# Second layers of eight chunks as seven block products, in a phase of their own

## The chip, the cores and the metric

The kernel runs on one core of a Trainium2 chip. TensorE multiplies matrices into PSUM, VectorE and ScalarE move and combine data, GpSimd does small element-wise work, and SyncE (SP) issues nearly all transfers between HBM and SBUF. The metric is the time of one execution in device microseconds (us), as a median of several runs, lower is better.

## What is computed

A linear attention with positive random features, followed by a gated two-layer network:

```python
def phi(x):
    proj = np.einsum('bhsd,df->bhsf', x, w_phi)
    proj = proj - np.max(np.abs(proj), axis=-1, keepdims=True)
    return np.concatenate([np.exp(proj), np.exp(-proj)], axis=-1)
q_p, k_p = (phi(q), phi(k))
kv = np.einsum('bhsf,bhsd->bhfd', k_p, v)
z = np.sum(k_p, axis=2)
num = np.einsum('bhsf,bhfd->bhsd', q_p, kv)
den = np.einsum('bhsf,bhf->bhs', q_p, z)[..., None] + 1e-06
x = (num / den).transpose(0, 2, 1, 3).reshape(4608, 512)
...
g = x @ w_gate
silu = g * (1.0 / (1.0 + np.exp(-g)))
val = x @ w_val
return (silu * val @ w_out).astype(np.float32)
```

Sizes: 8 batches, 8 heads, 576 tokens, head size 64, 128 features; then 4608 tokens, 512 inputs, 1536 hidden columns, 512 outputs. The three weight matrices arrive as 64-bit floats.

## The kernel before

**Numbers.** TensorE gets float32 operands in a form that is fast but keeps fewer bits (F32R). Each operand is split into a high part and a low remainder: ScalarE casts the high part (`copy` into `hh`, `xh`), VectorE subtracts (`hl`, `xl`). A product is then three matmuls: high by high, high by low, low by high.

**Tiling.** The 4608 tokens are 12 chunks of 384 (`CH`, `NCH`). The hidden columns are 12 groups of 128 (`NFT`, index `f`). For a chunk and an `f`, the first layer makes a gate and a value tile of 128 hidden columns by 384 tokens; tanh (ScalarE) and two VectorE operations make the hidden tile. The second layer (`second`, L864) takes 128 tokens of a hidden tile as the stationary operand and the 512 columns of `w2` for that `f` as the moving one, for three row tiles, and sums over `f` in three PSUM banks; behind `f` = 11 ScalarE copies a bank out (L905) and SP stores it.

**Stages.** Attention runs pair of heads by pair of heads (32 of them); its TensorE work goes ahead, and the network's matmuls fill the rest. Chunks 0 to 3 do their first layers directly (`first`, 24 matmuls of 384 columns for each `f`). Their sums for the block form below are made by `sums_of_weights` (L944).

Chunks 4 to 11 are taken in pairs by `pair` (L1054). Its first layer treats the two chunks, the two halves of the 512 inputs, and gate and value as a 2 x 2 block product, and makes it with seven block products instead of eight (products 0 to 6, line L1075, six matmuls of 384 columns each). `operands` (L1015) makes the seven left operands from four loads of `x_dram`, and `load_unit` (L999) fetches the weight blocks, in high and low, from `w1_dram` into six half buffers of `w1`, four loads for each `f`. The partial results live in two banks, `ps_gv`, with copies in `snap` (ScalarE L1083, VectorE L1086).

Pairs 4-5 and 6-7 are "narrow": between the products of the first layer stand the second layers of the first chunk only; the hidden tiles of the other chunk are stored in `h_dram` (`keep`, L843) and its second layers come behind the pair, from reloaded tiles. Pairs 8-9 and 10-11 are "wide": six banks hold the outputs of both chunks, whose second layers follow at once. `second` needs `w2_lo` for each `f`, reloaded by `parts_of_weights` (L788) into five buffers.

**Order.** All instructions are first collected as steps with costs and dependencies, and `Plan.run` (L101) lays them out ahead of time: on each engine the ready step of lowest rank goes first. Steps of the network on ScalarE, VectorE and SP mostly have the rank `FIRST`, preparations `NEXT`; TensorE's network products (`product`, L773) form one chain. `ahead(us)` holds a load back until that much planned TensorE work is left before its user. On the chip each queue is in order: a transfer that waits on SP holds back all transfers behind it.

**The early weights.** `weight_piece` (L350) turns the 64-bit weights into float32, splits them, and stores them: for the first layer the whole value (`w1_whole`) and both parts, for the second layer the low part (`w2_dram`); the high part of `w2` stays in SBUF (`w2_hi`).

Of the kernel before, what the change touches and what calls it, by code (L numbers as in the profile page):

```python
# [2 lines left out]

# [14 lines left out]
P = 128  # L18
# [31 lines left out]
NARROW = 2  # L50
AHEAD = (10, 8, 8, 20)
# [139 lines left out]
AT_ONCE = 2  # L191
# [28 lines left out]
def favor_attention_moe(ctx: ExitStack, tc: tile.TileContext, qT, kT, v, w_phi, wg, wv, wo, out):  # L220
# [8 lines left out]
    w2_dram = tc.dram_tile([NFT, P, DM], F32, name="w2_dram")  # L229
    h_dram = tc.dram_tile([NCH, NFT, P, CH], F32, name="h_dram")  # L230
# [10 lines left out]
    w2_hi = sb("w2_hi", [P, DM], F32R, NFT)  # L241
    w2_lo = sb("w2_lo", [P, DM], F32R, W2_SETS)
# [47 lines left out]
    hh, hl = sb("hh", [P, CH], F32R, 2), sb("hl", [P, CH], F32R, 2)  # L290
# [21 lines left out]
    ps_all = ps_o + work  # L312
# [37 lines left out]
    def weight_piece(f, layer, rank, over):  # L350
# [513 lines left out]
    def second(c, f, hidden, low, parts_of=range(NT), base=0, tail=None):  # L864
        b, ready = hidden
        readers, lo, lo_ready = low
        for t in parts_of:
            sl = slice(t * P, (t + 1) * P)
            o = ps_all[base + t]

            def go(t=t, sl=sl, o=o):
                if t == 0:
                    open_sum.append(f)
                    if f == NFT - 1:
# [5 lines left out]
                                            *(stored.get(base + t, ()) if f == 0 else ())])  # L880
# [8 lines left out]
            if n == NCH * NT - 1:  # L889
                for k, eng in enumerate(("ACT", "DVE")):  # L890
                    cols = slice(k * DM // 2, (k + 1) * DM // 2)

                    def copy(k=k, cols=cols, o=o):
                        if k:
                            nc.vector.tensor_scalar(out=tail[1][k](), in0=o[:, cols], scalar1=0.5, scalar2=None, op0=ALU.mult)
                        else:
                            nc.scalar.activation(tail[1][k](), o[:, cols], AF.Copy, scale=0.5)

                    cp = add(eng, act(DM // 2), copy, [done], FIRST)
                    q = nc.sync if k else nc.scalar  # L900
                    add("SP" if k else "ACT", P * DM * 2 if k else 60,
                        lambda q=q, k=k, cols=cols, rows=rows: q.dma_start(rows(cols), tail[1][k]()), [cp], FIRST)
                continue
            u = osb[n % len(osb)] if tail is None else tail[0][base + t]
            cp = add("ACT", act(DM), lambda o=o, u=u: nc.scalar.activation(get(u), o, AF.Copy, scale=0.5),  # L905
                     [done, out_done.get(n - len(osb)) if tail is None else None], FIRST)
            stored[base + t] = [cp]
# [12 lines left out]
    def tiles(c, f, hidden, low, base=0, tail=None):  # L920
        return [(c, f, hidden, low, range(t, t + 1), base, tail) for t in range(NT)]
# [50 lines left out]
    for c in range(EARLY, PAIRS):  # L972
        for f in range(NFT):
# [5 lines left out]
    ended = last["end"]  # L979
    x_half = lambda t, n: t[:, 2 * n:2 * n + 2]  # L980
    set2 = (PAIRS - 1) % X_SETS
    s0, s1_ = ((set2 + n) % X_SETS for n in (1, 2))
    op_hi = [x_half(xh[s0], 0), x_half(xh[s0], 1), x_half(xh[s1_], 0), x_half(xh[s1_], 1), view("m5", [2, CH], F32R, 1),
             x_half(xh[set2], 0), x_half(xh[set2], 1)]
    op_lo = [x_half(xl[s0], 0), x_half(xl[s0], 1), x_half(xl[s1_], 0), x_half(xl[s1_], 1), spare_lo,
             x_half(xl[set2], 0), x_half(xl[set2], 1)]
    snap = sb("snap", [P, CH], F32, 3)
    outs = [view("m2", [DM], F32, 2, DM * n) for n in range(2 * NT)]
    last_half = [view("m2", [DM // 2], F32, 2, 2 * NT * DM + n * DM // 2) for n in range(2)]

    op_free = [list(x_free[PAIRS - 3 + n]) for n in (0, 0, 1, 1)] + [list(early_done)] + [list(x_free[PAIRS - 1]) for _ in range(2)]
# [5 lines left out]
    held, loaded = {}, [0]  # L997

    def load_unit(f, j):  # L999
        u = UNITS[j]  # L1000
        g = u // 2
        if (f, g) not in held:
            first_ = 3 if g == 1 else 2 * g
            n = 2 * g + 2 - first_
            k = loaded[0] % len(slots)
            loaded[0] += 1
            after, slot_free[k] = slot_free[k], []
            stored_ = w_stored[f, 0 if g < 2 else g]
            held[f, g] = k, first_, add("SP", n * P * 4 * P * 4, lambda: nc.sync.dma_start(
                slots[k][:, :n].rearrange("p u h c -> p u (h c)").bitcast(F32), w1_dram[f, :, first_:first_ + n]),  # L1010
                [stored_, *after, ahead(AHEAD[2])], NEXT)
        k, first_, made = held[f, g]
        return slots[k][:, u - first_], slot_free[k], made

    def operands(c):  # L1015

        vec = nc.vector
        got = []
        for n in range(4):
# [6 lines left out]
                [*(x_stored[x] for x in need), *temp_free[n], ahead(AHEAD[3] - 2 * n)], NEXT))  # L1026
# [27 lines left out]
    def pair(c, wide, ready):  # L1054
# [3 lines left out]
        users = [[] for _ in range(7)]  # L1058
        held.clear()
        b_read, c_read = [gv_read[0]], [gv_read[1]]  # L1060
        bank_b, bank_c = ps_gv
        for f in range(NFT):
            job = list(waiting)
            waiting.clear()

            def mult(j, o, begin, final, after):
                w, free, made = load_unit(f, j)

                def go():
# [58 lines left out]
            if wide:  # L1128
                part(3)
# [104 lines left out]
```

## Time and profile before

| what | us |
|---|---|
| median of three runs | 1164.6 |
| lowest and highest of them | 1164.58 and 1167.27 |
| the profiled execution | 1165.77 |
| its span, first to last instruction | 1164.0 |
| TensorE busy, VectorE busy in it | 1149.0, 844.8 |
| ScalarE busy, GpSimd busy in it | 570.5, 136.2 |
| bytes moved, mean rate | 259.65 MB, 223 GB/s |

The profiled execution is one run with the hardware profiler on; all views of the trace are of it. In the profile PE is TensorE, PEld its weight loads, DVE VectorE, ACT ScalarE, POOL GpSimd, SPq the queue of SP. L12 is line 12 of the kernel. A row such as `DVE L859 hl<-m,hh` is an instruction of line 859 that writes the tile `hl` and reads `m` and `hh`; many tiles of the work space share the names `m` and `a`. "Idle before, releaser" is the time that the engine stood still before these instructions and what ended it.

### The profile page before, as it was taken

What the parts mean: (1) busy time and instruction counts of PE and PEld (TensorE: products, weight loads), DVE (VectorE), ACT (ScalarE), POOL (GpSimd) and SP (SyncE); (2) the same over time, 40 slices, a digit from 0 to 9 for tenths busy, and PEclk for the clock granted to TensorE, in tenths of its full rate; (3) what the DMA queues carried; (4) which work ended last, traced back from release to release, by engine and by line L of the source; (5) the groups of instructions that cost most, each with busy time, mean ns of one, the idle gap of its engine ahead of it and who ended that gap; (6) DMA issues with size and microseconds to landing.
All of it is one profiled execution on the core that took longest, in us unless ns stands there. A gap on an engine that the chain in (4) does not pass through costs nothing.

```text
span 1164.0 us, 23729 instructions
## 1 busy us (share of the span) xinstructions
PE 1149.0 (99%) x9201; PEld 999.4 (86%) x9201; DVE 844.8 (73%) x1397; ACT 570.5 (49%) x1166; POOL 136.2 (12%) x361
## 2 busy tenths in 40 slices
PE   9998999999999999999999999999999999999998
PEld 7776999998777878888888877899978999999997
DVE  6999999988888888898889986644445444654343
ACT  5665433336666656566656765422234223442233
POOL 1111000002233233323121120000000000000000
PEclk9999999999999999999999999999999999999999
DMA  6444877757787778888766756877788555765552
GB/s 182 109 128 161 310 271 262 262 197 219 230 256 250 251 251 288 276 274 297 245 187 188 224 161 207 274 264 239 239 267 283 187 182 180 235 237 191 178 188 94
DMA packets 141888, 259.65 MB, mean 223 GB/s; under 512 B 55376, under 2 KB 72784, under 8 KB 138704
## 3 DMA queue, kind: packets, MB, share of 16 engines
q1 hardware_dynamic: 141312, 257.87, 67.1%
q8 instruction: 73, 1.20, 0.4%
q14 instruction: 39, 0.32, 0.1%
q10 hardware_dynamic: 464, 0.26, 0.1%
HBM read 198.31 MB, written 59.77 MB: 222 GB/s over the span
## 4 chain that ended last, share of the span: by engine, by line
PE 86%; DVE 8%; DMA 2%; POOL 2%; issue 1%; SPq 1%; ACT 0%; POOLq 0%; DVEq 0%; ACTq 0%
PE gv L1075 30%; PE o L343 18%; PE gv L343 16%; PE work L343 11%; PE work L682 6%; PE work L518 5%; DVE m L494 1%; DVE km L489 1%; DVE m L590 1%; DVE km L585 1%; POOL rc L725 1%; DVE m L729 1%; DMA w_lo<-w_dram 1%; POOL rc L720 1%; DVE xl L756 0%
## 5 line engine op out<-in xcount | busy, mean ns | idle before, releaser
L1075 PE MATMUL gv<-xh,w 128*128 128x384 f32 x1152 | 325.4, 338 | 1.9 <-ACT snap L1083 1.7
L1075 PEld LDWEIGHTS gv<-xh,w 128*128 128x128 f32 x1152 | 211.1, 188 | 11.2 <-issue 2.8
L343 PE MATMUL gv<-xh,w 128*128 128x384 f32 x768 | 207.1, 338 | 3.0 <-DVE m L835 1.9
L1075 PE MATMUL gv<-xl,w 128*128 128x384 f32 x576 | 193.5, 336 | 0.0
L1086 DVE TENSOR_TENSOR snap<-gv,snap 128x384 f32<-128x384 f32 x144 | 80.2, 557 | 152.2 <-PE gv L1075 126.1
L343 PEld LDWEIGHTS gv<-xh,w 128*128 128x128 f32 x768 | 139.8, 188 | 7.7 <-DVE m L835 2.6
L343 PE MATMUL gv<-xl,w 128*128 128x384 f32 x384 | 128.9, 336 | 1.7 <-DVE xl L756 1.7
L1083 ACT COPY snap<-gv 128x384 f32<-128x384 f32 x144 | 68.4, 475 | 113.8 <-PE gv L1075 112.9
L343 PE MATMUL o<-w_hi,hh 128*128 128x512 f32 x288 | 115.1, 400 | 0.0
L343 PE MATMUL o<-w_hi,hl 128*128 128x512 f32 x288 | 113.0, 392 | 0.5 <-DVE hl L859 0.5
L343 PE MATMUL o<-w_lo,hh 128*128 128x512 f32 x288 | 113.2, 393 | 0.0
L1075 PEld LDWEIGHTS gv<-xl,w 128*128 128x128 f32 x576 | 108.2, 188 | 4.7
L682 PE MATMUL work<-m,m 128*32 128x288 f32 (+2 forms) x1280 | 80.3, 398 | 0.0
L343 PEld LDWEIGHTS gv<-xl,w 128*128 128x128 f32 x384 | 72.1, 188 | 3.3 <-DVE xl L756 2.3
L858 ACT CAST hh<-m 128x384 fp32r<-128x384 f32 x87 | 44.5, 512 | 53.1 <-DVE m L1099 29.6
L682 PEld LDWEIGHTS work<-m,m 128*32 128x32 f32 x1280 | 30.9, 110 | 41.7 <-issue 35.2
L343 PEld LDWEIGHTS o<-w_hi,hl 128*128 128x128 f32 x288 | 54.1, 188 | 13.7 <-DVE hl L859 1.6
L343 PEld LDWEIGHTS o<-w_hi,hh 128*128 128x128 f32 x288 | 54.1, 188 | 11.9 <-issue 5.1
L1093 ACT ACTIVATE m<-gv 128x384 f32<-128x384 f32 x48 | 23.6, 491 | 74.9 <-PE gv L1075 74.0
L343 PEld LDWEIGHTS o<-w_lo,hh 128*128 128x128 f32 x288 | 54.2, 188 | 6.4
L1094 DVE SCALAR_TENSOR_TENSOR m<-m,gv 128x384 f32<-128x384 f32 x48 | 26.4, 550 | 42.7 <-ACT m L1093 42.7
L1075 PE MATMUL gv<-m,w 128*128 128x384 f32 x192 | 57.2, 339 | 0.0
(190 smaller groups left out, 2189.4 us busy)
## 6 DMA issues: line engine op xcount, KB each, us to landing
w<-w_dram SPq DMA_DIRECT2D x144, 512.0 KB, 4.9
w_lo<-w_dram SPq DMA_DIRECT2D x108, 256.0 KB, 3.5
w_dram<-w SPq DMA_DIRECT2D x12, 1024.0 KB, 5.1
w_dram<-a SPq DMA_DIRECT2D x24, 512.0 KB, 4.0
w<-w_dram SPq DMA_DIRECT2D x12, 1024.0 KB, 6.6
w<-w_dram SPq DMA_DIRECT2D x48, 256.0 KB, 3.4
h_dram<-m SPq DMA_DIRECT2D x42, 192.0 KB, 2.0
m<-h_dram SPq DMA_DIRECT2D x36, 192.0 KB, 3.7
```

The source lines that it names most:

```text
L343: nc.tensor.matmul(o, l, r, start=a, stop=z)
L489: kmax = add("DVE", dve(n * NF), lambda m=m, view=view: vec.tensor_reduce(out=m, in_=view(), axis=AX.X, op=ALU.max, apply_absolute_value=T ...
L494: vec.tensor_tensor(out=room[:, :, 1], in0=view(), op=ALU.subtract, in1=m.rearrange("p (n o) -> p n o", o=1).broadcast_to([P, n, NF]))
L518: nc.tensor.matmul(ps_kv[r, n:n + (2 if tail else 1) * D2], x[:, r], y, start=g + m + k == 0, stop=tail and k == 1)
L585: mx = add("DVE", dve(u * NF), lambda u=u, m=m, view=view: vec.tensor_reduce(out=m[:, 4:4 + u], in_=view(), axis=AX.X, op=ALU.max, apply_a ...
L682: strips = lambda o, c, l, x, n, begin, final: nc.tensor.matmul(o[32 * n:32 * n + 32, c], l, x, start=begin, stop=final)
L858: s4 = add("ACT", act(CH), lambda: nc.scalar.copy(get(hh[b]), get(th[j])), [made, hid_free[b]], FIRST)
L1075: nc.tensor.matmul(o[:, :CH], l, r, start=begin and i == 0, stop=i == len(terms) - 1, skip_group_check=True)
L1083: return add("ACT", act(CH), lambda: act_.copy(snap[n], bank_b[:, :CH]), [after, *snap_free[n]], FIRST)
L1086: return add("DVE", dve(CH), lambda: vec.tensor_tensor(out=snap[n], in0=bank_c[:, :CH], in1=snap[n], op=ALU.add), after, FIRST)
L1093: t0 = add("ACT", act(CH), lambda: act_.activation(get(t_), get(x), AF.Tanh, scale=0.5), [*after, th_free[j]], FIRST)
L1094: t1 = add("DVE", dve(CH), lambda: vec.scalar_tensor_tensor(out=get(t_), in0=get(t_), scalar=1.0, in1=get(x), op0=ALU.add, op1=ALU.mult), ...
```

## The change

The second layers of chunks 4 to 11 leave the places described above.

- **Phase one** makes only first layers. `block` replaces `pair`: it is a generator of the seven products of one `f`, and `in_turn` runs two neighbouring blocks alternately on two pairs of banks (`ps_gv`, and two of the former output banks). Both chunks' hidden tiles go to `h_dram`. The order of the products changes a little (the fifth and fourth, the seventh and sixth trade places), and `snap` copies with it.
- **Shared weight loads.** `shared` lets chunks 8-9 run three `f` ahead (`LEAD`); from then on a block of chunks 8-9 and one of chunks 10-11 use the same loaded weights, and the last three `f` of chunks 10-11 stand alone. Each of the two pairs has its own operand buffers (`far`), in the room of `w2_hi`, `w2_lo`, the hidden tiles and the attention's tiles. Two further half buffers join the six (`more`).
- **Weights for phase two.** `weight_piece` also stores the whole value of `w2` (`w2_whole`). `sums_of_units` loads four 128-column blocks for each pair of `f`, GpSimd makes four differences, and SP stores them (`w2_sums`). `piece_of_weights` loads a 1536-column piece for each of the seven products and splits it; three pieces during phase one, four behind it.
- **Phase two.** `second_pair` handles two chunks as a 2 x 2 block product again: rows are the two chunks, the inner blocks are even and odd `f`, columns are the two interleaved sets of 128 output columns. It loads 24 hidden tiles, makes 24 sums and differences on GpSimd (`total`), splits 42 tiles (ScalarE and VectorE), and runs seven products of 2 x 6 x 3 matmuls with 384 moving columns. The weights are now the stationary operand, so the outputs come out with output columns on the partitions: TensorE transposes them back, four 128 x 128 blocks for each row tile (`turned`), and a copy and a store follow. Two sets of four banks alternate between pairs, and the lower chunk's transposes run inside the next pair's first product.
- At the very end a whole row tile of 512 columns is copied and stored, in place of two halves.

```diff
+    w2_whole = tc.dram_tile([NFT, P, DM], F32, name="w2_whole")
+    w2_sums = tc.dram_tile([4, P, NFT // 2, 2 * P], F32, name="w2_sums")
...
+            w_stored[f, 4 + layer] = add("SP", P * n * 4, lambda: nc.sync.dma_start(w2_whole[f], x()), [s6], rank)
+            wa_free[u].append(w_stored[f, 4 + layer])
...
+        p1 = mult(0, bank_b, True, False, b_read)
+        y1 = copy(0, bank_b, p1)
+        yield
+        p2 = mult(1, bank_c, True, True, c_read)
+        g1 = joined(0, bank_c, [p2, y1])
+        ja, ga = gate(snap[0], [g1])
+        snap_free[0] = [ga]
+        yield
...
+            else:
+                for x in (now, now, later_, now, later_, later_, now):
+                    step(x)
...
+        for f in range(LEAD, NFT):
+            held = {}
+            yield block(c_a, f, far_a, ready_a, held, f == 0, False)
+            yield block(c_b, f, far_b, ready_b, held, f == LEAD)
+        for f in range(LEAD):
+            yield block(c_b, f, far_b, ready_b, {}, False)
...
+        for o, l, r in ((4, 3, 1), (5, 1, 0), (6, 3, 5), (0, 2, 6)):
+            done = [add("POOL", POOLED, lambda o=o, l=l, r=r: gp.tensor_tensor(
+                out=sum_stage[:, o], in0=sum_stage[:, l], in1=sum_stage[:, r], op=ALU.subtract), done, NEXT)]
...
+        def split(name, q):
+            at, after = ring.pop(0)
+            x = tile_of[name, q]
+            hi = add("ACT", act(CH), lambda: act_.copy(get(at)[:, 0], x()), [made[name, q], *after], NEXT)
+            lo = add("DVE", dve(CH), lambda: vec.tensor_tensor(out=get(at)[:, 1], in0=x(), in1=get(at)[:, 0], op=ALU.subtract), [hi], NEXT)
...
+                        for m, (l, r) in enumerate(((hi, x[:, 0]), (hi, x[:, 1]), (lo, x[:, 0]))):
+                            nc.tensor.matmul(o[:, :CH], l, r, start=begin and q == 0 and m == 0, stop=q == NQ - 1 and m == 2,
+                                             skip_group_check=True)
...
+        p1 = mult(0, "a11", bb, True, b_free, flush)
...
+        y1 = [cp_(d, 0, bb, p1[d]) for d in range(2)]
+        p2 = mult(1, "a12", bc, True, c_free)
+        g1 = [jn_(d, 0, bc, [p2[d], y1[d]]) for d in range(2)]
...
+        p6 = mult(2, "s2", bb, False, [[x] for x in y1])
+        y2 = [cp_(d, 1, bb, p6[d]) for d in range(2)]
+        p5 = mult(3, "s1", bc, True, [[x] for x in g1])
+        y5 = [cp_(d, 2, bc, p5[d]) for d in range(2)]
+        p7 = mult(4, "s3", bb, False, [[x] for x in y2])
+        v2 = [jn_(d, 2, bb, [p7[d], y5[d]]) for d in range(2)]
+        p3 = mult(5, "s4", bc, False, [[x] for x in y5])
+        v1 = [jn_(d, 1, bc, [p3[d], y2[d]]) for d in range(2)]
...
+        p4 = mult(6, "a22", bb, False, [[x] for x in v2], last_)
+        y4 = [cp_(d, 3, bb, p4[d]) for d in range(2)]
...
+            for m, x in enumerate(blocks):
+                nc.tensor.transpose(bank[:, m * P:(m + 1) * P], get(x)[:, t * P:(t + 1) * P], ident)
```

The holding-back times change too: `AHEAD[2]`, that of the weight blocks, goes from 8 to 10 us, and the operands' from 20 to 18, 50 and 35.

More of the change, by code (lines that the diff above doesn't have):

```diff
@@ L2 @@
 from contextlib import ExitStack
+from itertools import chain
 import concourse.bass as bass
@@ L190 @@
 SLOW = 2.0
-AT_ONCE = 2
 NEXT_KEYS = 0
@@ new lines, in in_turn @@
+    def in_turn(blocks):
+        now = None
+        for later_ in chain(blocks, [None]):
+            step = lambda x: x is None or next(x)
+            if now is None:
+                for _ in range(3):
+                    step(later_)
+                    if waiting:
+                        second(*waiting.pop(0))
+            else:
+                for x in (now, now, later_, now, later_, later_, now):
+                    step(x)
+            now = later_
+    for c in (PAIRS, PAIRS + 2):
+        ready = operands(c, near, SOON[0])
+        blocks = [block(c, f, near, ready, {}, f == 0) for f in range(NFT)]
+        if c == PAIRS:
+            in_turn(blocks)
@@ new lines, in favor_attention_moe, with turned, go @@
+    sets_free = [[list(ended)] * 3 + [list(stored[2])], [list(x) for x in (*bank_read[0], *bank_read[1])]]
+    late_jobs = []
+    def turned(c, name, blocks, bank, after, cols=slice(0, DM), engines=("ACT",)):
+        t, k = name
+        free, made = after
+        n = len(blocks)
+        def go():
+            for m, x in enumerate(blocks):
+                nc.tensor.transpose(bank[:, m * P:(m + 1) * P], get(x)[:, t * P:(t + 1) * P], ident)
+        s = product(n * 108, go, [*free, *made])
+        i = taken[0] % len(whole)
+        taken[0] += 1
+        u = whole[i]
+        at = lambda: u()[:, :n * P]
+        eng = engines[t % len(engines)]
+        cp = add(eng, act(n * P), lambda: (nc.scalar.copy(at(), bank[:, :n * P]) if eng == "ACT" else
+                                           nc.vector.tensor_copy(at(), bank[:, :n * P])), [s, *whole_free[i]], FIRST)
+        whole_free[i] = [add("SP", P * n * P * 4, lambda: nc.sync.dma_start(
+            out[c * CH + t * P:c * CH + (t + 1) * P, cols], at()), [cp], FIRST)]
+        return s, cp
@@ L1171, in favor_attention_moe, with grab @@
-    put_off()
+        which = index % 2
+        bb, bc = sets4[which][:2], sets4[which][2:]
+        b_free, c_free = sets_free[which][:2], sets_free[which][2:]
+        tile_of, made = {}, {}
+        def grab():
+            return exact.pop(0)
+        for name, chunk, e in (("a11", c, 0), ("a21", c + 1, 0), ("a22", c + 1, 1), ("a12", c, 1)):
+            for q in range(NQ):
+                at, after = grab()
+                tile_of[name, q] = at
+                made[name, q] = add("SP", P * CH * 4, lambda at=at, chunk=chunk, f=2 * q + e: nc.sync.dma_start(at(), h_dram[chunk, f]),
+                                    [h_kept[chunk, 2 * q + e], *after, ahead(SOON[3] - 1.5 * len(made))], NEXT)
```

448 lines of the change are left out of this document (299 added, 149 removed).

## The prediction

> **What bounds the kernel now.** I read the page first: busy time, slices, chain.
>
> ```profile
> span 1164.0 us, 23729 instructions
> PE 1149.0 (99%) x9201; PEld 999.4 (86%) x9201; DVE 844.8 (73%) x1397; ACT 570.5 (49%) x1166; POOL 136.2 (12%) x361
> PEclk9999999999999999999999999999999999999999
> PE 86%; DVE 8%; DMA 2%; POOL 2%; issue 1%; SPq 1%; ACT 0%; POOLq 0%; DVEq 0%; ACTq 0%
> ```
>
> TensorE is busy throughout at full clock and 86% of the chain is its work: every matmul that goes or comes moves the end, unless a new wait appears. A busy share says nothing of a matmul's price, because matmuls overlap; I take that from the chain in order of time (start, duration, what), where the first product of each hidden block recurs, and from the sums by stretch (engines' busy us, then clock, DMA share, GB/s).
>
> ```profile
> 167.20 12.51 PE gv L343 x72
> 181.77 12.51 PE gv L343 x72
> 740.23 5.25 PE gv L1075 x30
> 843.78 5.24 PE gv L1075 x30
> 856.61 2.75 DMA m<-h_dram
> 860.64 6.06 DMA w_lo<-w_dram
> 902.60 3.13 PE gv L1075 x18
> 1144.36 3.14 PE gv L1075 x18
> 740.00:850.00 110.00, 110.00 (x597) 105.66 (x597) 47.91 (x92) 34.27 (x74) 0.00 (x0) 1.00 0.75 252
> 850.00:900.00 50.00, 47.15 (x225) 40.44 (x224) 25.16 (x41) 21.30 (x39) 0.00 (x0) 1.00 0.83 285
> 902.60:1144.40 241.80, 241.80 (x1262) 225.41 (x1262) 112.70 (x201) 79.00 (x161) 0.00 (x0) 1.00 0.59 194
> ```
>
> From 740.23 to 843.78 lie 11 blocks of a narrow pair: 9.414 us each, for 42 matmuls of 384 columns and 9 of 512. From 902.60 to 1144.36 lie 21 blocks of wide pairs: 11.512 us, for 42 and 18. The difference is nine 512-column matmuls in 2.098 us, **233 ns each**; the 42 then take 7.316 us, **174.2 ns each**. Both stretches have TensorE full. Between them TensorE lacks 2.85 us (47.15 of 50), where chunk 7's second layers run alone and the chain waits for h_dram and w_lo loads.
>
> **The change, part by part.** *Products.* Eight chunks lose 8 x 12 x 3 x 3 = 864 matmuls of 512 columns: 201.4 us. Four pairs gain 7 products x 2 halves x 6 x 3 = 252 each, 1008 of 384 columns: 175.6 us. The outputs come out transposed, so each pair adds 6 row tiles x 4 = 24 transposes, 96 in all. The early stage has the same operation on float32:
>
> ```profile
> L601 PE MATMUL o<-ident,m x38: 272/273/328, 12.1 to 93.8; 128*128 128x128 f32 x38
> 23.75 0.82 PE L601 MATMUL o<-ident,m 128*128 128x128 f32 x6
> 24.40 1.03 PE L343 MATMUL gv<-wbd,m 128*128 128x256 f32 x4
> ```
>
> One lasts 273 ns, but six start within 24.40 - 23.75 = 0.65 us, 108 ns each: 96 cost 10.4 us. Sum: -201.4 + 175.6 + 10.4 = **-15.4 us**. The Trainium skill ("TensorE: Matmul & The Clock Gate", Part 4: PE-mode transpose) gives about 275 ns for a transpose in a kernel's context. By that figure 96 would be an estimated 26.4 us and nearly all of the gain gone; this trace agrees with it as a duration, not as a price in a row.
>
> *The lone second layers* of chunk 7 go, and with them the 2.85 us: -2.9. What would be late next there are the weight loads, and those are priced below. Chunk 5's lie beside attention with TensorE full: nothing.
>
> *The end.*
>
> ```profile
> 1159.76 0.40 PE L343 MATMUL o<-w_hi,hl 128*128 128x512 f32 x1
> 1161.06 0.33 SPq L902 DMA_DIRECT2D out_dram<-m  x1
> out_dram<-m SPq DMA_DIRECT2D x25, 256.0 KB, 2.4
> L905 ACT ACTIVATE m<-o 128x512 f32<-128x512 f32 x18 | 10.6, 599 | 2.7 <-PE o L343 2.3
> L1083 ACT COPY snap<-gv 128x384 f32<-128x384 f32 x144 | 68.4, 475 | 113.8 <-PE gv L1075 112.9
> ```
>
> Today 3.8 us follow the last matmul (1160.16 to 1164.0): two half copies, an issue, a 128 KB landing. Afterwards: a 384-column copy 0.48, the transposes (counted above) with 0.2 to drain the last, a 512-column copy 0.60, issue 0.33, 2.4 landing, the same 0.7 behind it and some 0.2 of signals: 4.9. With 0.4 for the third upper tile, which waits for the first one's copy out of the same bank, +1.5.
>
> *First layers without second layers between them.* The rows are a join, that group and the last matmuls of attention.
>
> ```profile
> L1086 DVE TENSOR_TENSOR snap<-gv,snap 128x384 f32<-128x384 f32 x144 | 80.2, 557 | 152.2 <-PE gv L1075 126.1
> L1075 PE MATMUL gv<-xh,w 128*128 128x384 f32 x1152 | 325.4, 338 | 1.9 <-ACT snap L1083 1.7
> 720.09 3.05 PE work L682 x48
> ```
>
> The new order interleaves two blocks on two pairs of banks, so a product that needs a copy of its bank has two others (2.1 us) ahead of it; copy plus join is 0.48 + 0.56. That I cost at nothing, as TensorE idles 1.9 us in all before the 1152 matmuls of L1075's largest group today; without that cover each block would lose about 1 us. DMA is another matter. A narrow block moves 1.835 MB of weights (three loads of 512 KB, one of 256), one 192 KB store and 256 KB of w_lo: 2.294 MB in 9.414 us, 244 GB/s. A block now moves 1.835 + 2 x 0.197 = 2.228 MB in 7.316 us: **305 GB/s**, by the row of 740 to 850 a DMA share of 0.75 x 305/252 = 0.91. Blocks that share weights need half of that. By 723, when attention ends, about 122 us of these products have run today (12 x 9.414 + 12 x 2.1 = 138 until 740, less 17); that is 16 to 17 of the new blocks, and of the 30 unshared ones (24, three before and three behind the shared stretch) some 14 remain to run with no attention beside them. The landings, for 740 to 850 and for 860 to 892 (309 GB/s at a share of 0.88), and SP's own waits:
>
> ```profile
> 860.00:900.00 40.00, 37.77 (x181) 32.65 (x182) 20.18 (x31) 17.36 (x31) 0.00 (x0) 1.00 0.88 309
> w<-w_dram SPq DMA_DIRECT2D x33, 512.0 KB, 5.8
> w<-w_dram SPq DMA_DIRECT2D x8, 512.0 KB, 7.1
> SPq L1009 <- PE gv L1075: 216.9, 110, 3.1
> h_dram<-m SPq DMA_DIRECT2D x42, 192.0 KB, 2.0
> ```
>
> There are six half buffers. Counted in products of 1.045 us, a block's four loads hold one for 3, 4, 7 and 1; of 6 x 7 = 42 that leaves 27, so 6.75 products or 7.05 us from release to need. At 5.8 + 0.33 issue nothing is lost; at 7.1 + 0.33 a block takes 7.43/7.05 x 7.316 = 7.70, 0.38 more, over 14 blocks 5.3 us. The demand is nearest to the row of 0.88, so I take **+5.3**; ends 0, and 21 if only 252 GB/s is had (8.84 us a block). On SP the queue is in order: behind a weight load that waits for its half buffer (3.1 us at longest) stand both stores of h, where one stood before; behind those the th buffers, ScalarE's tanh, and the copies behind it in ScalarE's order. 3.1 + 2.0 is under a block's 7.3, so they stay hidden as long as loads aren't late too.
>
> *The second phase itself.* A pair is 252 x 0.1742 + 24 x 0.108 = 46.5 us of TensorE. Beside it lie 42 splits (ScalarE 0.51, VectorE 0.56), 8 bank copies or joins each, six output copies, and 24 sums on GpSimd:
>
> ```profile
> L859 DVE TENSOR_TENSOR hl<-m,hh x87: 501/551/1090, 123.1 to 1156.3; 128x384 fp32r<-128x384 f32 x87
> L731 DVE TENSOR_TENSOR m<-m x32: 745/752/1202, 25.4 to 739.1; 128x576 f32<-128x576 f32 x32
> L952 POOL TENSOR_TENSOR m<-m x48: 727/740/1722, 262.4 to 553.0; 128x256 f32<-128x256 f32 x48
> 442.46 1.05 DVE L731 TENSOR_TENSOR m<-m 128x576 f32<-128x576 f32 x1
> 443.44 1.09 DVE L859 TENSOR_TENSOR hl<-m,hh 128x384 fp32r<-128x384 f32 x1
> 442.16 2.96 POOL L952 TENSOR_TENSOR m<-m 128x256 f32<-128x256 f32 x3 [4.46 <-DMA m<-w_whole]
> L958 DVE TENSOR_TENSOR a<-m,a x24: 641/684/704, 285.8 to 562.6; 128x512 fp32r<-128x512 f32 x24
> L858 ACT CAST hh<-m 128x384 fp32r<-128x384 f32 x87 | 44.5, 512 | 53.1 <-DVE m L1099 29.6
> ```
>
> ScalarE and VectorE have some 28 us of their own, under 46.5. But where a VectorE subtraction meets a GpSimd one they exclude each other: L859 takes 1.09 for 0.55 while three GpSimd sums take 2.96 for 2.22. The Trainium skill ("SBUF — State Buffer", Who interferes with whom) says that a VectorE instruction with two SBUF inputs and a GpSimd one that reads SBUF block each other for the whole instruction. The trace agrees that one waits for the other.
> So 42 splits and 24 sums share one turn. A sum of 384 columns, scaled from 740 ns at 256, is 1.11 us. At full durations 26.6 + 23.4 = 50.0 us a pair, 3.5 over, 14 in all, and the last four weight pieces (12 VectorE subtractions of 0.684) add 8.2: 22 at most. In that meeting, though, 3 x 0.74 + 0.75 + 0.55 = 3.52 us of nominal work ran from 442.16 to 445.12, in 0.84 of it: 42.0 a pair, under 46.5, and over it only in the first (42.0 + 6.9). The row is nearer: **+2.5**; ends 0 and 22.
>
> *The switch.* The third product needs s2, 12.5 us into the phase. Its buffers come free at the end of phase one, and 12 sums take 13.3 us, but each step needs one sixth: 0 to 2 us late, **+1**. The last four weight pieces form a chain: a 768 KB load, near 6 us by the row of 5.8 for 512, then three splits at VectorE's 0.68, some 8 us each. They are wanted at 18.8 us (three products of 36 matmuls) and every 6.3 after; four are made by 32 and the last is wanted at 37.6. The first three and the weight sums run beside first layers, where today's rows from 740 on show GpSimd idle and VectorE under half busy: nothing.
>
> *The early store* of whole w2 blocks the next piece's buffer, but a weight block recurs every 14.57 us (167.20, 181.77), TensorE filling it: nothing, at worst 3.
>
> Sum: -15.4 - 2.9 + 1.5 + 5.3 + 2.5 + 1.0 = **-8.0 us**. The profiled execution took 1165.8, 1.8 beyond its span; the median is 1164.6, and I put the difference on the median: **1156.6**.
>
> **Rivals.** *All covered*: loads land in time and the turns fit: -15.4 - 2.9 + 1.5 = -16.8, **1147.8**. For it: every interleaving distance is long. Against: 0.91 is beyond any stretch of 40 us here.
>
> *The shared turn decides, and the kernel gets slower*: VectorE's splits and GpSimd's sums exclude each other for their full durations in the second phase, TensorE waits for splits: 22 in place of 2.5, +11.5, **1176**. It decides where it costs 8.0 + 2.5 = 10.5 over the four pairs: (4 x 46.5 + 10.5 - 6.9)/4 = 47.4 us of shared turn a pair. Against it: 0.84 above.
>
> *Loads bind the first phase* at the narrow stretch's 252 GB/s: 21 for 5.3, **1172**. Against: 309 GB/s over 40 us.
>
> *The switch stalls*: SP's order holds a22 or a weight piece back by one product and a landing, about 10 us in place of 1: **1166**.
>
> *Transposes don't overlap*: 273 for 108 ns, +15.8, **1172**. The rows speak against it. The section on PE-mode transpose in the Trainium skill is what would lead there.
>
> **How the numbers follow.** Forecast 0.52, its own range 1151 to 1162; all covered 0.22; shared turn 0.07; loads bind 0.07; switch 0.10; transposes 0.02. From 1146 to 1165 lie the forecast, all covered and part of the switch case, eight in ten. About 0.3% is what a measurement of this kernel can tell from no change, here 3.5 us. Faster than that: 0.52 + 0.22 less a little, 0.73. Within: that little and the switch, 0.12. Slower: 0.15.
>
> **What would show it.** The 42 matmuls of a first-layer block in 7.3 us, or 7.7 with TensorE idle and a weight load named as releaser; 512 KB landings at 6 to 7 us; second-phase pairs 46.5 us apart, the first some 3 longer, with splits stretched past 0.6 where GpSimd is busy; 108 ns between transposes; 4.9 us behind the last product. I am wrong if TensorE's busy time falls by something else than about 15 us, or if it idles in the second phase for splits over 10 us.

## The result: slower by 1.2%, and the profile after

The changed kernel takes 1179.55 us (median of 4 runs, 1178.79 to 1181.62) against 1165.93 before on the same chip: a ratio of **1.0117, 95% interval 1.0093 to 1.0142**. The forecast was 1156.6, faster. The profiled execution took 1179.03 us. First its page: the span, the engines' busy time, the granted clock in 40 slices, and the chain by engine.

```profile
span 1177.2 us, 25148 instructions
PE 1146.7 (97%) x9441; PEld 1026.9 (87%) x9441; DVE 962.9 (82%) x1514; ACT 629.2 (53%) x1290; POOL 278.0 (24%) x481
PEclk9999999999999999999999999999999999899999
PE 79%; DVE 13%; DMA 3%; issue 2%; ACT 1%; POOL 1%; SPq 0%; DVEq 0%; POOLq 0%; ACTq 0%
```

TensorE's part of the chain fell from 86% to 79% and VectorE's rose from 8% to 13%: some of what was TensorE's own pace is now waiting. The sums by stretch (busy us of PE, PEld, DVE, ACT, POOL; then clock, DMA share, GB/s) and the rows at which each pair of the new phase begins say where.

```profile
507.00:965.00 458.00, 451.96 (x3655) 415.04 (x3654) 355.29 (x592) 238.15 (x508) 72.69 (x163) 1.00 0.82 269
800.00:850.00 50.00, 50.00 (x288) 49.85 (x288) 31.18 (x54) 17.56 (x37) 9.85 (x12) 1.00 0.83 264
965.00:1028.00 63.00, 50.60 (x263) 46.78 (x262) 60.47 (x65) 30.32 (x66) 50.98 (x40) 0.92 0.44 140
1028.00:1076.00 48.00, 46.99 (x281) 46.61 (x279) 37.16 (x48) 28.20 (x58) 29.47 (x25) 1.00 0.40 132
```

```profile
964.85 0.51 PE L1352 MATMUL work<-spare_lo,xh 128*128 128x384 f32 x2
1028.15 0.60 PE L1352 MATMUL gv<-hidden,xh 128*128 128x384 f32 x2
1075.98 0.59 PE L1352 MATMUL work<-spare_lo,xh 128*128 128x384 f32 x2
1123.91 0.59 PE L1352 MATMUL gv<-hidden,xh 128*128 128x384 f32 x2
```

Where TensorE is fed, the new products have the predicted price: 288 in 50 us, 174 ns each. But the first pair of the last phase takes 63.3 us and the next two 47.8 and 47.9, against 46.5 of work. In those 63 us VectorE is busy for 60.5 and GpSimd for 51.0, with 40 instructions, while a pair has only 24 sums: GpSimd is already at the second pair's. Its rows from 960.62 on count 24 sums up to the first one below; the second one begins another 20 in this stretch (timeline: start, duration, line; in brackets the idle time before it).

```profile
989.70 1.43 POOL L1325 TENSOR_TENSOR w_last<-w_last,w_last 128x384 f32<-128x384 f32 x1
998.22 2.43 POOL L1325 TENSOR_TENSOR spare<-spare,w_last 128x384 f32<-128x384 f32 x2 [7.08 <-DVE m L1206]
```

The rest of the loss lies ahead of 964.85. To divide it I took every matmul's time from its start to the next one's start, by line, from 507.0, where first layers by blocks begin in both kernels:

| us from 507.0 on | before | after | change | predicted |
|---|---|---|---|---|
| second layers and attention's projections (L343; L347) | 232.4 | 26.6 | -205.8 | -204.3 |
| first-layer products (L1075; L1085) | 356.7 | 367.6 | +10.9 | +5.3 |
| second-phase products (L1352) and waits among them | 0 | 189.9 | +14.3 over 175.6 | +3.5 |
| transposes (L1290) and waits among them | 0 | 18.1 | +7.7 over 10.4 | 0 |
| attention's other matmuls | 63.7 | 63.7 | 0 | 0 |

(The -204.3 holds the lone second layers, the +3.5 the shared turn and the switch.) So about 22 us were lost in the last phase and 11 before it. The waits of TensorE in the first pair, and VectorE and GpSimd there (timeline: start, duration, line):

```profile
PE work L1290 <- DVE m L1367: 4.6, 1, 4.6
PE work L1352 <- DVE m L1334: 4.1, 3, 2.5
```

```profile
970.34 1.37 DVE L1334 TENSOR_TENSOR m<-w_last,m 128x384 fp32r<-128x384 f32 x1
974.21 4.36 DVE L1206 TENSOR_TENSOR w_hi<-a,w_hi 128x512 fp32r<-128x512 f32 x3
984.88 3.98 DVE L1334 TENSOR_TENSOR m<-w_last,m 128x384 fp32r<-128x384 f32 x3
984.50 5.24 POOL L1325 TENSOR_TENSOR m<-m,w_last 128x384 f32<-128x384 f32 x4
```

A split's subtraction (L1334), 0.55 us in the kernel before (L859 there), takes 1.33 to 1.37; a weight piece's (L1206) 1.45; a sum on GpSimd 1.31. They alternate, one for one. In the first-layer phase the chain stands at 790, and there it doesn't name the weight loads:

```profile
780.86 6.21 DMA x_dram<-m
787.09 4.23 DMA spare<-x_dram
792.08 0.48 ACT snap L1095
```

The operands of chunks 10 to 11 are prepared from attention's last rows, which go to DRAM and come back. ScalarE's cast of them (L1044) waits for the reload until 791.3, and a block's copy of its bank (L1095) stands behind it in ScalarE's order, so TensorE waits too. TensorE's waits for such copies from 507 to 965 (total, times, longest):

```profile
PE gv L1085 <- ACT snap L1095: 2.1, 2, 1.9
PE o L1085 <- ACT snap L1095: 1.2, 3, 0.6
```

All waits that the list names for first-layer products come to 4.8 us, 1.9 before; what else they lost lies in a half clock and in longer steps between matmuls. Some of the shorter waits stand at 645 to 661, beside the preparation of chunks 6 to 7. Around such waits the granted clock is half for a stretch of 3.41 us or twice that (clock is the third figure from the end):

```profile
793.70:797.11 3.41, 3.41 (x13) 3.41 (x12) 2.88 (x5) 0.48 (x1) 0.00 (x0) 0.51 1.03 409
981.40:984.81 3.41, 3.31 (x9) 2.35 (x9) 3.41 (x4) 1.93 (x4) 3.41 (x4) 0.50 0.83 297
1018.90:1025.73 6.83, 3.14 (x12) 3.14 (x13) 4.83 (x7) 1.68 (x3) 2.75 (x3) 0.50 0.14 54
```

In the kernel before, the clock fell only at its very end. The Trainium skill ("TensorE: Matmul & The Clock Gate", Part 1: The HAM clock gate) gives a free-running window of 3413 ns and half clock after an idle one; the trace agrees on the 3.41 us, but not on the idle window: the fall at 793.7 came after 1.9 us of standing still.

### The profile page after: what moved, and what is told of

Read it like the earlier page. It is cut to its first block, busy times and chain, and to the rows that moved or that the text cites. A ratio compares the mean times of both kernels' runs of the same rounds, so it can differ in the third digit from the quotient of the medians.

```text
span 1177.2 us, 25148 instructions
## 1 busy us (share of the span) xinstructions
PE 1146.7 (97%) x9441; PEld 1026.9 (87%) x9441; DVE 962.9 (82%) x1514; ACT 629.2 (53%) x1290; POOL 278.0 (24%) x481
## 4 chain that ended last, share of the span: by engine, by line
PE 79%; DVE 13%; DMA 3%; issue 2%; ACT 1%; POOL 1%; SPq 0%; DVEq 0%; POOLq 0%; ACTq 0%
PE gv L347 17%; PE gv L1085 14%; PE o L1085 13%; PE o L347 9%; PE work L688 6%; PE work L347 5%; PE work L524 5%; PE gv L1352 4%; PE o L1352 3%; PE work L1352 3%; DVE m L1334 2%; DMA spare<-x_dram 1%; DMA x_dram<-m 1%; DVE m L500 1%; DVE km L495 1%
## 5 line engine op out<-in xcount | busy, mean ns | idle before, releaser
L347 PE MATMUL gv<-xh,w 128*128 128x384 f32 x768 | 208.3, 340 | 2.6 <-DVE m L841 1.5
L347 PEld LDWEIGHTS gv<-xh,w 128*128 128x128 f32 x768 | 140.8, 189 | 7.4 <-issue 2.3
L347 PE MATMUL gv<-xl,w 128*128 128x384 f32 x384 | 129.5, 337 | 1.7 <-DVE xl L762 1.7
L347 PE MATMUL o<-w_hi,hidden 128*128 128x512 f32 x288 | 100.7, 398 | 0.0
L1085 PE MATMUL gv<-xh,w 128*128 128x384 f32 x288 | 85.7, 341 | 0.6 <-ACT xh L1044 0.4
L1085 PE MATMUL o<-xh,w 128*128 128x384 f32 x288 | 85.0, 340 | 0.8 <-ACT snap L1095 0.6
L1085 PE MATMUL gv<-m,w 128*128 128x384 f32 x358 | 76.8, 337 | 0.0
L347 PEld LDWEIGHTS gv<-xl,w 128*128 128x128 f32 x384 | 72.7, 189 | 3.2 <-DVE xl L762 2.2
L347 PEld LDWEIGHTS o<-w_hi,hidden 128*128 128x128 f32 x288 | 54.0, 188 | 13.3 <-issue 3.3
L1085 PEld LDWEIGHTS gv<-m,w 128*128 128x128 f32 x358 | 63.5, 188 | 1.1 <-issue 0.5
L1085 PEld LDWEIGHTS gv<-xh,w 128*128 128x128 f32 x288 | 53.0, 188 | 5.0 <-issue 3.3
L347 PE MATMUL o<-w_lo,hidden 128*128 128x512 f32 x144 | 56.6, 393 | 0.0
L1085 PEld LDWEIGHTS o<-xh,w 128*128 128x128 f32 x288 | 52.9, 188 | 3.4 <-issue 1.4
L1095 ACT COPY snap<-o 128x384 f32<-128x384 f32 x72 | 34.3, 476 | 38.7 <-PE o L1085 17.2
L943 POOL TENSOR_TENSOR m<-m 128x256 f32<-128x256 f32 x48 | 37.7, 786 | 65.9 <-DMA a<-in_kT_dram 21.7
```

The costliest lines, as they stand in the source:

```text
L347: nc.tensor.matmul(o, l, r, start=a, stop=z)
L943: done = [add("POOL", POOLED, lambda o=o, l=l, r=r: gp.tensor_tensor(out=x(o), in0=x(l), in1=x(r), op=ALU.subtract), done, rank)]
L1085: nc.tensor.matmul(o[:, :CH], l, r, start=begin and i == 0, stop=i == len(terms) - 1, skip_group_check=True)
L1095: return add("ACT", act(CH), lambda: act_.copy(snap[n], bank[:, :CH]), [after, *snap_free[n]], FIRST)
```

## Experiments

Ratios are to the kernel before, run beside each on the same chip. Theory A: VectorE's splits and GpSimd's sums exclude each other, and this is the loss of the last phase. Rival B: VectorE is simply full in the first pair. Rival C: the loads and weight pieces at the switch come late. Rival D: the sums come late whoever makes them.

**1. All sums on VectorE.**

```diff
-            pool_ = True
+            pool_ = False
```

> The 24 sums of each second-phase pair move from GpSimd to VectorE, nothing else. Theory A (the shared turn: VectorE's splits wait for GpSimd's sums, 1.36 for 0.55 us each, and the clock falls behind the stalls): splits fall back to about 0.56 us, the first pair from 63 to 48 to 50 us, the clock stays at 1.0 in the second phase, the whole from 1179.5 to about 1163. Theory B (VectorE is simply full in the first pair, 100% from 970 to 1020): 24 more instructions of 0.55 make that pair longer still by up to 13 us, about 1185. Theory C (the switch: loads and weight pieces come late): the sums don't matter, 1177 to 1180.

Measured: ratio 1.0010 (0.9996 to 1.0024), span 1164.5. The splits' row (min/median/max ns), the waits of the first pair, and the starts of the first two pairs:

```profile
L1334 DVE TENSOR_TENSOR m<-w_last,m x39: 547/557/561, 973.9 to 1145.1; 128x384 fp32r<-128x384 f32 x39
```

```profile
PE work L1352 <- DVE spare_lo L1334: 5.2, 1, 5.2
```

```profile
965.43 0.51 PE L1352 MATMUL work<-spare_lo,xh 128*128 128x384 f32 x2
1017.93 0.59 PE L1352 MATMUL gv<-hidden,xh 128*128 128x384 f32 x2
```

No split exceeds 0.56 us, although VectorE now makes 24 sums more a pair. The first pair falls from 63.3 to 52.5 us, the others to 46.6, and the 96 transposes make 95 steps of together 10.3 us, 109 ns each. Some 12 us were the shared turn, and B and C fall: they had a longer first pair, or no change. Theory A had 48 to 50 us for the first pair and no fall of the clock, and that missed: what is left of its surplus is one wait of 5.2 us and a half clock behind it.

**2. The same with GpSimd kept busy.** Each sum on VectorE is followed by one or two GpSimd subtractions of 256 columns from it, which nobody reads.

```diff
+            for _ in range(2 if q % 2 else 1):
+                add("POOL", pool2(256), lambda: nc.gpsimd.tensor_tensor(
+                    out=wbd, in0=tile_of[o, q]()[:, :256], in1=tile_of[o, q]()[:, :256], op=ALU.subtract), [made[o, q]], NEXT)
```

> As the run with the sums on VectorE, and GpSimd subtracts 36 times 256 columns a pair of a fresh sum from itself into a scratch tile that nobody reads: about the same GpSimd time as in the changed kernel, but no result of GpSimd is waited for in this phase. Theory A (shared turn): splits are stretched again to about 1.0 to 1.4 us where GpSimd is busy and most of the loss comes back, 1172 to 1185. Theory D (the sums of GpSimd came too late for the splits): nothing waits for GpSimd, so it stays at the time of the run with the sums on VectorE alone.

Measured: ratio 1.0185 (1.0157 to 1.0214). The first row is the same split, the second the largest group of the added instructions:

```profile
L1337 DVE TENSOR_TENSOR m<-w_last,m x39: 540/546/966, 979.3 to 1165.1; 128x384 fp32r<-128x384 f32 x39
```

```profile
L1328 POOL TENSOR_TENSOR wbd<-w_last 128x256 f32<-128x256 f32 x57 | 47.1, 826 | 21.3 <-DVE w_last L1325 17.3
```

Splits reach 0.97 us again (67 of all 168 take more than 0.6 us, and 55 of the 96 sums on VectorE too), and the kernel is 1.75% slower than 1 for instructions that give nothing to anyone; at 1188.7 us the loss is larger than theory A said. D falls: GpSimd's activity costs by itself, not the lateness of its results.

**3. Half of the sums (s3, s4) on GpSimd.** `pool_ = o in ("s3", "s4")`.

> Only s1 and s2 move to VectorE; s3 and s4 stay on GpSimd. Theory A: half the meetings, splits stretched in part of each pair only, first pair some 54 to 56 us, the whole about 1168 to 1171. Theory B: up to 6 us longer than the changed kernel.

Measured: 1.0008 (0.9990 to 1.0026), better than theory A said. The first pair took 50.8 us, the others 46.6: from the second pair on, twelve sums a pair fit beside the splits.

**4. Operands of chunks 10 to 11 made later**, behind the first block of chunks 8 to 9 (with `LEAD = 4`).

```diff
+                ready_b.extend(operands(c_b, far_b, 0))
```

> The operands of chunks 10-11 are planned behind the first block of chunks 8-9 (and those lead by four blocks instead of three), so that ScalarE's casts of them no longer stand ahead of a bank copy while the last attention output is stored and reloaded. Theory E (that wait of 1.9 us at 790 and the half clock of 3.4 us behind it cost some 4 us of phase one): no TensorE wait there, no fall of the clock at 794, about 1175.5. Rival F (weight loads are what phase one loses its 10 us to): the same or up to 1 us slower, as one block pair less shares its loads.

Measured: 1.0116 (1.0085 to 1.0147), no change, as rival F said. The wait at 790 and its half clock went, and a wait for weight loads of 2.5 us came (`w<-w_dram`); the first-layer products took 366.5 for 367.6 us.

**5. Splits ranked first**, ahead of sums and weight pieces, all sums on VectorE (`NEXT - 0.1` for both halves of a split).

> All 24 sums of each pair on VectorE as in e1, and the second-phase splits (the ScalarE cast and the VectorE subtraction of the low part) ranked ahead of the sums and of the weight pieces' subtractions. Theory (what is left of e1's loss in the phase at the end is the order on VectorE: the first pair took 52.5 us against 46.6 for the others, with 5.2 us of TensorE waiting for one low part that stood behind sums and weight pieces): the first pair comes down to 47 to 48.5 us, the wait of 5.2 and the fall of the clock behind it go, the whole is 5 to 6 us under e1: about 1161.5, ratio 0.995 to 0.997. Rival (the low part is late because the weight pieces' loads, or the first-layer outcomes themselves, come late): the same wait under another name, the first pair at 51 to 53 us, ratio 1.000 to 1.002.

Measured: 1.0009 (0.9994 to 1.0023), as experiment 1 and as the rival said. The first pair took 50.3 us, between the two expectations, and 2.8 us of waiting for a split stayed. I read this as splits whose operand isn't made yet, which gain nothing by being ranked first. The profiled execution took 1172.0 us, 4.6 over this kernel's median, and its first-layer phase 462.7 against 457.7 in 1, so its stages can't be set beside those of 1 to a few microseconds.

**6. Two preparations left out.** Chunks 6 to 7 and 10 to 11 use the operands of the pair before them; those chunks compute something else.

```diff
-        ready = operands(c, near, SOON[0])
+        ready = operands(c, near, SOON[0]) if c == PAIRS else ready
```

> The changed kernel without the operand preparations of chunks 6 to 7 and 10 to 11: these chunks use the operands of 4 to 5 and of 8 to 9 again, so the outputs of these chunks are another computation's. Theory (the first-layer phase lost its 10.7 us at the preparations of operands, which the second layers used to cover, and not at the loads of weights): the gaps at about 650 and 790 go, no half clock at 794, the first-layer phase shortens by 5 to 8 us, the whole is 1171 to 1175, ratio 1.004 to 1.008. Rival (the phase is longer because the weights of the block products come late or the products themselves are slower): the phase keeps its 457.8 us within 1.5, the ratio stays at 1.010 to 1.013.

Measured: 1.0131 (1.0115 to 1.0147). The gaps at 650 and the half clock at 794 went as expected, and the phase became no shorter, so the theory missed: 506.4 to 966.08 (second fence). TensorE's waits there moved to VectorE's work for attention and to weight loads:

```profile
PE work L347 <- DVE m L500: 1.7, 1, 1.7
PE o L1085 <- DMA w<-w_dram: 1.4, 2, 0.8
PE gv L1085 <- DMA w<-w_dram: 1.1, 3, 0.6
```

```profile
966.08 0.52 PE L1353 MATMUL work<-spare_lo,xh 128*128 128x384 f32 x2
```

**7. Other buffers for the operands**, so that no preparation writes where the chunks before still read (sums and splits as in 5; chunks 6 to 7 take the set `far[0]`, 8 to 9 the set `near`).

> e5 with the operand buffers exchanged: chunks 6 to 7 have a set of their own, prepared 40 us ahead, chunks 8 to 9 take the set that chunks 4 to 5 leave. Theory (TensorE stands for about 3 us at 645 to 661 because the operands of chunks 6 to 7 are written into the buffers that chunks 4 to 5 still read): that gap goes, the first-layer phase is 2 to 4 us shorter than in e5, the pairs at the end stay at 46.6 to 48.5 us; about 1158.5, ratio 0.992 to 0.995. Rival (the gap only moves to chunks 8 to 9, which now are the ones written into buffers just read): the same time as e5 within 1 us.

Measured: 1.0007 (0.9994 to 1.0021), no gain. In the profiled execution, 3.8 us over the median, the waits at 645 to 661 are gone, but one of 2.1 us ends at 643.2, again for a bank copy behind the preparation of operands, and the phase took 465.8 us. So 4 and 6 take a wait away, 7 moves one, and none makes the phase clearly shorter.

**8. Half of the weight bytes.** Loads into the six half buffers bring high parts only; chunks 4 to 11 compute with low parts that lay there.

```diff
-                get(slots[k])[:, :n].rearrange("p u h c -> p u (h c)").bitcast(F32), w1_dram[f, :, first_:first_ + n]),
+                ... if k > 5 else nc.sync.dma_start(get(slots[k])[:, :n, 0].bitcast(F32), w1_dram[f, :, first_:first_ + n, :2 * P]),
```

> The changed kernel, but the loads of first-layer weights into the six half buffers bring the high parts only (half of the bytes; the low parts are what lay there), so the outputs of chunks 4 to 11 are another computation's; every instruction and every wait stays. Theory W (what is left of the loss of 10.7 us in the first-layer phase is the load on DMA: a share of 0.81 to 0.84 against 0.70 before, with x_dram stores of 6.2 and reloads of 4.2 us at 781 to 791 and late weights as soon as another wait is gone): landings shorten, the gap at 790 shrinks, the phase of 457.8 us shortens by 2 to 6, ratio 1.006 to 1.010. Rival V (the phase waits for VectorE and ScalarE, which attention keeps busy, and DMA only looks full): the phase within 1.5 us of 457.8, ratio 1.010 to 1.013.

**9. Both, 6 and 8.**

> The last two together: operand preparations of chunks 6 to 7 and 10 to 11 left out and half of the weight bytes, outputs of chunks 4 to 11 another computation's. Leaving out the preparations alone changed nothing (phase 459.5 us; TensorE then waited 2.5 us for weight loads, and for attention's VectorE work). Theory (two limits one behind the other, preparations and weight loads): now the phase shortens by 5 to 9 us to 449 to 453, ratio 1.003 to 1.007. Rival (the loss is spread over waits for attention's VectorE and ScalarE work): 456 to 460, ratio 1.010 to 1.014.

Measured: 1.0083 (1.0064 to 1.0101) for 8 and **1.0055 (1.0036 to 1.0074)** for 9. First and last time of the phase, of 8 and then of 9 (its first row, the start of the last phase, and the phase's sums):

```profile
L1086 PE MATMUL gv<-xh,w x288: 333/334/522, 508.1 to 780.3; 128*128 128x384 f32 x144
961.92 0.51 PE L1353 MATMUL work<-spare_lo,xh 128*128 128x384 f32 x2
```

```profile
L1086 PE MATMUL gv<-xh,w x288: 333/334/446, 507.2 to 774.0; 128*128 128x384 f32 x144
955.39 0.51 PE L1354 MATMUL work<-spare_lo,xh 128*128 128x384 f32 x2
507.00:955.00 448.00, 446.80 (x3653) 414.13 (x3652) 336.57 (x565) 227.25 (x492) 75.40 (x163) 1.00 0.64 196
```

The phase lasts 457.9 us in the changed kernel, 459.6 without the preparations, 453.8 with half of the bytes, and 448.2 without both. Single profiled executions scatter: in 1, 3 and 5, whose first-layer phase does the same work, it took 457.7, 461.0 and 462.7 us. The 4.1 us of 8 are no more than that, and the interval of its ratio overlaps that of the changed kernel; the 9.7 us of 9 are more, and 13 and 14 below, which leave out the same two, took 447.8 each. In 9 the first-layer products take 358.3 us, nearly the 356.7 of the kernel before: the loss of the phase is these two together, and I read it as one limit behind the other. (The first pair took 65.9 us for 63.3, so that 9.7 us less there became 7.2 in the whole.)

**10. The product of gate and value on GpSimd** (sums and splits as in 5).

```diff
-            return add("DVE", dve(CH), lambda: vec.tensor_tensor(out=get(th[j]), in0=get(th[j]), in1=snap[n], op=ALU.mult), after, FIRST)
+            return add("POOL", pool2(CH), lambda: nc.gpsimd.tensor_tensor(out=get(th[j]), in0=get(th[j]), in1=snap[n], op=ALU.mult), after, FIRST)
```

> The splits-first kernel (all sums on VectorE, splits ranked first), with the product of gate and value of every first-layer block (96 multiplications of two SBUF tiles of 384 columns) on GpSimd in place of VectorE. Theory (VectorE, busy 0.88 of the time while attention runs, sets the pace of attention and of the preparations): 0.55 us less VectorE work per chunk and block, attention ends some 5 us earlier, first-layer phase 2 to 5 us shorter, ratio 0.996 to 0.999. Rival (a GpSimd product of about 1.05 us takes its turn from VectorE as in the phase at the end, so VectorE gains nothing and the h stores come later): phase the same or up to 5 us longer, ratio 1.001 to 1.005.

Measured: 1.0092 (1.0072 to 1.0111): a loss beyond what the rival said. Attention did end earlier, at 762.7 against 780.6 in 5, but the phase grew from 462.7 to 473.3 us, with TensorE waiting 8.5 us for copies out of its banks. What it cost there I didn't take apart.

**11 and 12. A lead of four blocks**, on 5 and on 3 (`LEAD = 4`).

> The splits-first kernel (all sums on VectorE, ratio 1.0009) with chunks 8 to 9 one block further ahead of chunks 10 to 11 before the two share weight loads (four in place of three). Theory (what is left of the loss is the first-layer phase; one of its waits is for the operands of chunks 10 to 11, whose x_dram store and reload end at 791 while the products want them at 790): the products want them 7.3 us later, the wait of 1.9 us and the 1.7 us of half clock behind it go, two blocks more load their weights alone, which costs under 1 us; the first-layer phase is 2 to 4 us shorter, ratio 0.997 to 0.999. Rival (the phase is full on both counts, so the gain comes back as waits for weight loads, as when the operands were made later): ratio 1.000 to 1.002.

> The kernel with half of the sums on GpSimd (s3 and s4; ratio 1.0008) with the same lead of four blocks. Theory: as in the run beside it, 2 to 4 us under its own counterpart, and the pairs at the end stay at 50 to 51, then 46.6 us: ratio 0.996 to 0.999. Rival: the gain comes back as waits for weight loads: 1.000 to 1.002.

Measured: 1.0039 (1.0021 to 1.0056) and 1.0040 (1.0025 to 1.0054), slower than their counterparts; theory and rival missed in both. The chain of 11 shows that the lead left the cast where it was, before the same bank copies, as early as the reload allowed:

```profile
781.31 6.18 DMA x_dram<-m
787.50 4.50 DMA spare<-x_dram
792.02 0.84 ACT m L1044
```

What is wanted later isn't made later: the operands are queued ahead by a fixed distance. The loss shows in the last phase: the first pair grew from 50.3 to 55.3 us in 11, with 5.0 us of waiting for splits, and from 50.8 to 54.6 in 12; why is open.

**13. All three taken out**: 9 with all sums on VectorE. **14. No sums at all**: 9, and in the last phase each product takes the tile that its sum would have read first, so these outputs are another computation's.

> Preparations of chunks 6 to 7 and 10 to 11 left out, half of the weight bytes (outputs of chunks 4 to 11 another computation's), and all sums of the phase at the end on VectorE. Theory (the three causes are the whole of the difference, and they add up): 1179.5 - 9.8 - 11.7 = 1158, first-layer phase 447 to 449 us, first pair 52 to 53, the others 46.6; ratio 0.991 to 0.994. Rival (a wait that is taken out of one phase comes back in the other, as half clock or as late operands of the first pair): 1162 to 1167, ratio 0.996 to 1.000.

> As the run beside it, but with no sums at all in the phase at the end: the products take the tiles that the sums would have read first, so the outputs are another computation's once more. Theory S (the 4 to 6 us that the first pair still loses are VectorE's time for sums ahead of splits): all pairs at 46.6 to 47.5 us, 4 to 6 us under the run beside it, ratio 0.986 to 0.989. Rival P (they belong to the weight pieces, whose loads and splits come late): first pair 51 to 53 as with sums, ratio as the run beside it.

Measured: 0.9978 (0.9968 to 0.9987) and **0.9863 (0.9846 to 0.9879)**; medians 1164.16 and 1150.46 us. The starts of the first two pairs, of 13, its waits there, and then of 14 with the first pair's sums:

```profile
956.57 0.51 PE L1354 MATMUL work<-spare_lo,xh 128*128 128x384 f32 x2
1015.34 0.60 PE L1354 MATMUL gv<-hidden,xh 128*128 128x384 f32 x2
```

```profile
PE work L1354 <- DVE w_lo L1336: 4.9, 2, 3.1
PE work L1354 <- DVE spare_lo L1336: 4.2, 1, 4.2
```

```profile
953.89 0.52 PE L1355 MATMUL work<-spare_lo,xh 128*128 128x384 f32 x2
1000.85 0.59 PE L1355 MATMUL gv<-hidden,xh 128*128 128x384 f32 x2
954.00:1001.00 47.00, 45.87 (x266) 45.22 (x265) 35.37 (x69) 32.82 (x69) 0.00 (x0) 1.00 0.62 209
```

The causes do not simply add up, and the rival of 13 holds: in 13 the first-layer phase keeps its gain (508.8 to 956.57), but the first pair lasts 58.8 us, 6.3 more than in 1: two thirds of the gain come back as waits for splits at the switch. I read this as VectorE having the same sums, splits and weight pieces ahead of it while TensorE arrives earlier. Without sums (14) that pair lasts 47.0, with the weight pieces still there. So the surplus of the first pair belongs to the sums, on whichever engine, as theory S said, though it had 4 to 6 us for them and 14 is 13.7 under 13; and the kernel stands at 1150.5, near the 1147.8 that the prediction gave for a change whose additions are all covered.

None of the kernels that compute the whole is measurably faster than the kernel before; the nearest are 7, 3, 5 and 1.

## Why the prediction was wrong

*The products and transposes: right.* 174 ns and 109 ns, where TensorE is fed (50 us with 288 products; experiment 1). The exchange does save its 15 us of work, and 14 shows it, with the two preparations, half of the weight bytes and the sums left out.

*The lone second layers and the end: right.* 205.8 us went against 204.3. Behind the last matmul lie 4.1 us against 3.8 before, and 0.5 us of copy ahead of the last transposes.

*The shared turn, +2.5: the step that failed.* The ratio behind it held: a split of 0.56 us and a sum of 1.01 alone take 1.31 together, 0.83 of their sum, where I had 0.84. What failed was the averaging, "42.0 a pair, under 46.5, and over it only in the first (42.0 + 6.9)". It gave each pair its own 24 sums. Nothing holds GpSimd to that: as long as tiles are free it goes on to the next pair's sums, so 40 of them stood against the first pair's 42 splits and 12 weight pieces. While both queues are full, each VectorE subtraction costs one full exchange of 1.3 us, not its share of an average. By my own ratio that is (42 x 0.55 + 12 x 0.684 + 40 x 1.01) x 0.84 = 60.2 us, and VectorE was busy 60.5 (some 5 of that on bank joins and the last first-layer tiles, so the nearness is partly luck). With the pair's own 24 sums the same working gives an estimated 46.7 us, as long as TensorE's 46.5. But no run keeps GpSimd to its own pair's sums: that sums cost is shown by 1, 2 and 14, the part of running ahead is counted and not tested. The surplus of the phase, 22.0 us (14.3 + 7.7, the switch and the half clock in it), equals by chance the price of the rival "the shared turn decides", which had full durations in every pair; here 16.8 of it fell on the first. That rival had a chance of 0.07.

The page behind that rival, in the Trainium skill ("SBUF — State Buffer", Summary: rules for kernel authors), has the second of the two to issue blocked until the first finishes. The alternation agrees with it; the sum of the two durations, 1.57 us, does not agree with the 1.31 measured.

*The first-layer phase, +5.3 for loads of weights and nothing for bank copies: wrong in form and place.* No wait of TensorE in the changed kernel is put down to a weight load, so the sign I had named didn't come; that half of the bytes gave 4.1 us back is near the 5.3, but by luck. What TensorE does wait for are the bank copies, which I had cost at nothing because two other products, 2.1 us, lie ahead of each: a copy that stands in ScalarE's queue behind a cast, and that cast behind a reload, comes later than that. I read it so: operand preparations used to run beside lone second layers, which want no bank copies; when these were gone, a late cast held up a block's copy. The waits named are less than half of the 10.9 us, so how the rest arises stays open. I had asked what the removed second layers' own waits cost (-2.9) and not what they had covered.

*The switch, +1: about right in the changed kernel.* Its third product waits 1.1 and 0.5 us for splits:

```profile
979.89 0.44 PE L1352 MATMUL work<-m,xh 128*128 128x384 f32 x1 [1.11 <-DVE m L1334]
981.17 0.53 PE L1352 MATMUL work<-w_lo,xh 128*128 128x384 f32 x1 [0.49 <-DVE w_lo L1334]
```

It is where VectorE makes the sums as well that this place costs more: the 5.2 us of experiment 1 and 4.2 of the 9.1 us of 13 are the third product's low parts, behind sums and weight pieces in VectorE's one queue. The other 4.9 us of 13 stand in the first product; 1.8 of them end with a split that stood behind a weight piece, whose load landed at 961.63 (chain of 13):

```profile
956.76 4.87 DMA a<-w_sums
```

*Not foreseen:* the half clock around waits. The three stretches above last 13.65 us, so at most 6.8 us are due to it, 5.1 of them in the first pair. (A further 3.41 us at 111.0 lie ahead of 507.0, where the two kernels are level.)

*Signs.* Two that the prediction named came true. TensorE's busy time fell by 2.3 us (1149.0 to 1146.7) and not by some 15 (longer steps and half clock count as busy); and in the first pair it stood 12.4 us, 7.7 of them for splits and 4.6 for a bank join behind splits in VectorE's queue.

## What to carry to other kernels

Price contention by what meets in time, not by the average of a stage: an engine with nothing to wait for runs ahead, and its work falls on the first, fullest stretch. Work that is moved to the end also stops covering something; ask of each preparation beside it what stood between it and the busy engine. When two limits lie one behind the other, taking out either may show nothing clear of noise, so test both together before calling a cause refuted.

## What the hardware showed unexpectedly

- A VectorE subtraction of two SBUF tiles (384 columns, 0.56 us alone) and a GpSimd one (1.01 alone) alternate in 1.31 us, and subtractions of 512 columns (0.69 alone) take 1.45 in such company. GpSimd work that nobody reads slows VectorE too: 1.75% of the whole in experiment 2.
- The granted clock fell to 0.5 for 3.41 us at 793.7, after a wait of only 1.9 us from 790.7 to 792.6, and for 6.83 us from 1018.9, 0.9 us into the wait of 4.6. The length of a wait doesn't decide it alone: in 1 and 3 waits of 1.9 and 2.7 us at the same place, before 794.2 and 793.6, were followed by full clock.
- An x_dram store of 288 KB and its reload of 384 KB took 6.21 and 4.23 us; the phase's medians are 5.2 and 5.0 at a DMA share of 0.82, and 3.1 and 4.1 at 0.64 (experiment 9).
